# Zero fills behind weights and rows, and the routing table inside the early down product, in an FFT-convolution and mixture-of-experts kernel

## The chip, the core and the metric

One core of one Trainium2 chip runs the kernel. The metric is the device time of one execution in microseconds. The kernel before took 543.51 us, the median of three runs (543.25 to 544.37).

Engines are named TensorE (PE, with its weight loads as PEld), VectorE (DVE), ScalarE (ACT), GpSimd (POOL) and SyncE (SP, which here only issues transfers). Each works through its own instructions in order, and waits at the first one whose inputs or buffers are not ready.

## What is computed

The input is x of 8 batches x 3072 rows x 256 columns, float32. Each batch is convolved with a filter along its rows by Fourier transforms, and the result, 24576 rows, goes through a mixture of eight experts:

```python
X = np.fft.rfft(x, axis=1)
y = np.fft.irfft(X * F, n=x.shape[1], axis=1)     # attn_out
logits = rows @ w_gate                             # rows: y as (24576, 256)
expert_idx = np.argmax(logits, axis=1)             # one expert for each row
# each expert takes its first 768 rows in order; the others' output stays zero
h = np.maximum(np.einsum('ecd,edf->ecf', disp, w1), 0.0)
y = np.einsum('ecf,efd->ecd', h, w2)
out[i] = gate_w[i] * y[expert_idx[i], pos[i]]      # kept rows only
```

Eight experts take 768 rows each, so 6144 of 24576 output rows are written by an expert and all others are zero. In general the first three batches (9216 rows) fill every expert; the kernel convolves those three, and a branch on a flag convolves the others only if an expert is not yet full.

## The kernel before, in words

**Convolution of a batch.** A transform of 3072 points is done as 96 x 32. The steps `a` (input product, line 216) write ZA, `t` (transposes, line 225) write Q. Then `middle` (line 293) runs over six groups g of four frequency pairs: `b(g, h)` for the two column halves h makes a product of Q with constants on TensorE (line 242), multiplies it by the filter on VectorE (t1 and t2, line 258) and combines on GpSimd (lines 262 and 263); `catch_up` then runs `g` on the groups that are complete (line 275, with its two splits on ScalarE and VectorE, lines 278 and 279) and one step later `bi` (line 289, copied into V by ScalarE at line 291). The matmuls of line 275 in group g need the combinations of group g - 1. VectorE transposes V (`ti`, line 333), and `ai` (line 335) makes the inverse product from it in steps of three or four columns, whose results go through the tile rt (five buffers) to ybuf in memory by a store on SyncE's queue (line 350). The first of the two column halves also gives the logits L (line 349).

**Order of the work.** The instructions are written out by hand in the order in which each engine gets them. `middle` takes two lists of other work: `first`, inverse steps left over from the batch before, and `fill`, of which one entry is run between the two halves of each group from g = 1 on and one behind its `catch_up`, ten places in all. `interleave` mixes lists.

**Routing** (`route`, line 367) of a batch: counts (f0 to f5 and the matmul f6), slot numbers (`slots`), four one-hot masks (`onehot`, VectorE) and the table: 32 small matmuls (line 455) that accumulate the token of each slot, added to `tacc` (lines 460 and 461).

**Three batches.** The loop at line 700 does batch 0 and 1: four input loads for the next batch, four zero fills (`zero_out`, 2 MB each from the tile zt to the output, on SyncE), the middle, then the inverse product of this batch mixed with the input product of the next. Batch 2 follows at line 720. Its middle also carries the start of expert 0: pools for weights and rows are opened on the memory of the convolution's input (`side_ctx.close()`), w1 of expert 0 is loaded into `raw` (line 726) before the zero fills, and its splits into a high and a low part are put into fill places 0 to 3 (ScalarE and GpSimd, 512 columns each); fill place 4 holds the load of w2 of expert 0 into the same buffer (`loads[1]`, a pool of one buffer) and `early_rows`, which gathers the first 384 rows of expert 0 from batches 0 and 1 (three indirect transfers issued by GpSimd) and adds their logits; the splits of w2 (ScalarE and VectorE) follow in places 6 to 9. `early_turn` transposes the rows at the end.

**From there to the branch.** Behind batch 2's middle, up steps of expert 0 (`early`, line 754, six matmuls of line 515 each) are mixed with the inverse product (`first`, `rest`), then counts, the flag (`full_flag`: a matmul, a minimum and a cast on VectorE), slots and masks, the down product of the 384 rows (`down`, 24 matmuls of line 564 for each 128 rows, a scaled copy on ScalarE and a scatter by GpSimd), the table, and the gather of expert 0's other 384 rows (`load_rows`, line 780). All engines then load the flag into a register (line 785) and branch (line 786).

**The experts.** The loop at line 852 goes over the experts with TensorE nearly always busy: up product, down product, transposes of the next rows (`prep`), while the next expert's weights are loaded (ScalarE's queue) and split, and its rows gathered. In front of it stand `prep` of expert 0's second 384 rows and `scatter_rows`.

## Time and profile before

| | |
|---|---|
| median of three runs | 543.51 us (543.25 to 544.37) |
| the profiled execution | 547.82 us, of which 546.1 us from the first to the last instruction (the span) |
| TensorE matmuls busy | 496.4 us, 91% of the span |
| VectorE, ScalarE, GpSimd busy | 251.7, 253.0 and 238.5 us |
| mean granted TensorE clock | 0.970 of full speed |
| transfers | 81.27 MB, 149 GB/s in the mean |

Times in the profile's rows are microseconds from the span's start, and those of the prediction's steps are on the same clock. A row of a timeline gives start, duration, engine, line, operation, destination and sources, the count of merged instructions, and in brackets how long the engine had been idle and what ended that. L12 is line 12 of the kernel before. Some matmul records can be missing, and fp32 matmuls show as two records each.

### The profile page before, as it was taken

How to read it: one execution, taken by the hardware profiler on the slowest of the kernel's cores; microseconds unless marked ns; L12 is line 12 of the kernel's file. 1: busy time of each engine (PE TensorE's matmuls, PEld its weight loads, DVE VectorE, ACT ScalarE, POOL GpSimd, SP SyncE). 2: the span in 40 equal slices, each digit the busy share in tenths (PEclk: the TensorE clock that was granted, in tenths of full speed). 3: DMA queues.
4: the chain of work that ended last, by engine and by line, in shares of the span. 5: the costliest groups of instructions: out<-in, count | busy, mean ns of one | idle time of the engine just before them, and what ended most of it. 6: DMA issues, size and time to landing. Idle time of an engine off the chain costs nothing.

```text
span 546.1 us, 9913 instructions
## 1 busy us (share of the span) xinstructions
PE 496.4 (91%) x3836; PEld 489.2 (90%) x3836; DVE 251.7 (46%) x536; ACT 253.0 (46%) x599; POOL 238.5 (44%) x241
## 2 busy tenths in 40 slices
PE   7999999999997709889489999999999999999992
PEld 6889999999997709889389999999999999999992
DVE  0197743987437706757236325234242442323500
ACT  3435767356673406753154635436254362453410
POOL 2165010550106534206466946658458474582021
PEclk9999999999999958999699999999999999999997
DMA  8999662994629940161264216033170250601010
GB/s 220 306 334 406 215 184 60 314 407 134 183 59 331 401 127 1 45 180 44 71 191 151 95 50 225 30 128 118 44 231 20 80 176 32 228 24 49 0 37 22
DMA packets 52918, 81.27 MB, mean 149 GB/s; under 512 B 3968, under 2 KB 31872, under 8 KB 52736
## 3 DMA queue, kind: packets, MB, share of 16 engines
q1 hardware_dynamic: 39072, 52.90, 30.0%
q10 hardware_dynamic: 9184, 14.68, 8.3%
q0 software_dynamic: 4608, 12.98, 7.0%
q8 instruction: 32, 0.52, 0.4%
q14 instruction: 22, 0.18, 0.1%
HBM read 39.07 MB, written 41.48 MB: 148 GB/s over the span
## 4 chain that ended last, share of the span: by engine, by line
PE 37%; issue 8%; POOL 3%; DMA 2%; POOLq 0%; ACT 0%
PE ps L515 18%; PE ps L564 17%; DMA rows<-ybuf,idxg 2%; POOL y L568 2%; PE ps L486 1%; POOL rows L475 1%; POOL wbl L656 0%; POOLq L906 0%; ACT wbh L655 0%; POOL wal L656 0%; ACT h L492 0%; POOLq L568 0%; POOLq L475 0%; POOLq L785 0%; POOLq L786 0%
## 5 line engine op out<-in xcount | busy, mean ns | idle before, releaser
L564 PE MATMUL ps<-wbh,h 128*128 128x256 f32 x768 | 139.2, 281 | 0.0
L564 PEld LDWEIGHTS ps<-wbh,h 128*128 128x128 f32 x768 | 118.6, 188 | 0.0
L498 DVE SCALAR_TENSOR_TENSOR h<-ps,h 128x384 fp32r<-128x384 f32 x120 | 66.8, 558 | 91.1 <-ACT h L492 91.1
L564 PE MATMUL ps<-wbl,h 128*128 128x256 f32 x384 | 107.7, 280 | 0.0
L568 POOL DMA_INDIRECT y<-ob,idxs x48 | 49.0, 1020 | 91.2 <-ACT ob L567 89.4
L515 PE MATMUL ps<-xh,wah 128*128 128x384 f32 x256 | 86.9, 340 | 0.1
L515 PE MATMUL ps<-xl,wah 128*128 128x384 f32 x256 | 86.7, 339 | 0.0
L492 ACT ACTIVATE h<-ps 128x384 fp32r<-128x384 f32 x128 | 62.8, 493 | 51.3 <-PE ps L515 50.6
L515 PE MATMUL ps<-xh,wal 128*128 128x384 f32 x256 | 86.4, 337 | 0.0
L564 PEld LDWEIGHTS ps<-wbl,h 128*128 128x128 f32 x384 | 72.2, 188 | 0.0
L567 ACT ACTIVATE ob<-ps,gt 128x256 f32<-128x256 f32 x48 | 22.5, 473 | 82.2 <-PE ps L564 60.1
L275 PE MATMUL ps<-IG,t 128*128 128x136 f32 x288 | 40.1, 287 | 20.7 <-POOL t L263 20.7
L275 PEld LDWEIGHTS ps<-IG,t 128*128 128x128 f32 x288 | 36.6, 195 | 22.0 <-POOL t L263 21.9
L262 POOL TENSOR_TENSOR t<-t,t 128x256 f32<-128x256 f32 x33 | 24.9, 753 | 70.0 <-DVE t L258 62.0
L475 POOL DMA_INDIRECT rows<-ybuf,idxg x45 | 45.3, 1007 | 18.6 <-issue 9.5
L515 PEld LDWEIGHTS ps<-xh,wah 128*128 128x128 f32 x256 | 48.3, 189 | 0.5 <-ACT xh L492 0.5
L515 PEld LDWEIGHTS ps<-xl,wah 128*128 128x128 f32 x256 | 48.3, 189 | 0.3 <-DVE xl L500 0.3
L515 PEld LDWEIGHTS ps<-xh,wal 128*128 128x128 f32 x256 | 48.3, 189 | 0.0
L344 PE MATMUL ps<-V,AI 128*96 128x144 f32 (+1 forms) x384 | 46.6, 277 | 1.4 <-DVE V L333 1.4
L656 POOL TENSOR_TENSOR wal<-raw,wah 128x1024 fp32r<-128x1024 f32 (+1 forms) x18 | 39.0, 2182 | 19.4 <-issue 11.9
L344 PEld LDWEIGHTS ps<-V,AI 128*96 128x96 f32 x384 | 45.2, 160 | 1.9 <-ACT full L495 1.7
L500 DVE TENSOR_TENSOR xl<-ps,xh 128x384 fp32r<-128x384 f32 x32 | 16.2, 547 | 63.9 <-ACT xh L492 63.9
(118 smaller groups left out, 788.4 us busy)
## 6 DMA issues: line engine op xcount, KB each, us to landing
y<-zt SPq DMA_DIRECT2D x12, 2048.0 KB, 19.1
raw<-w ACTq DMA_DIRECT2D x14, 1024.0 KB, 7.1
xt<-x SPq DMA_DIRECT2D x20, 384.0 KB, 5.2
ybuf<-rt SPq DMA_DIRECT2D x30, 162.0 KB, 2.4
ybuf<-rt SPq DMA_DIRECT2D x24, 192.0 KB, 2.7
raw<-w SPq DMA_DIRECT2D x2, 1024.0 KB, 10.3
V<-x SPq DMA_DIRECT2D x4, 384.0 KB, 8.7
AI<-cai SPq DMA_DIRECT2D x1, 1536.0 KB, 12.5
```

The costliest lines, as they stand in the source:

```text
L262: eng.tensor_tensor(out=t1[:, :, 0, :], in0=t1[:, :, 0, :], in1=t2[:, :, 1, :], op=ALU.subtract)
L275: nc.tensor.matmul(ps[:, i * 136:(i + 1) * 136], self.ysb[(p // 4, h)][:, (p % 4) * 128:(p % 4 + 1) * 128], self.IG[:, h, :], start=True, ...
L344: nc.tensor.matmul(ps[:N1, i * w:(i + 1) * w], AI[:, n0 + i, :], V[h][:, :, n0 + i, :], start=True, stop=True)
L475: nc.gpsimd.indirect_dma_start(out=rows[:, t, :], out_offset=None, in_=yrows[:lim, :], in_offset=bass.IndirectOffsetOnAxis(ap=idx[:, j + t ...
L492: nc.scalar.activation(out=hi, in_=ps, func=f)
L498: nc.vector.scalar_tensor_tensor(out=lo, in0=ps, scalar=0.0, in1=hi.bitcast(F32), op0=ALU.max, op1=ALU.subtract)
L500: nc.vector.tensor_tensor(out=lo, in0=ps, in1=hi.bitcast(F32), op=ALU.subtract)
L515: nc.tensor.matmul(ps[:, :n * 128], w[:, kk, m * 128:(m + 1) * 128], y[:, kk, o], start=k == 0, stop=k == 5)
L564: nc.tensor.matmul(ps[:, :D], y[:, m, o], w[:, m, :], start=m == 0 and j == 0, stop=m == NF - 1 and j == 2)
L567: nc.scalar.activation(out=ob, in_=ps[:, :D], func=AF.Copy, scale=gt[:, i:i + 1])
L568: ins = nc.gpsimd.indirect_dma_start(out=out, out_offset=bass.IndirectOffsetOnAxis(ap=(idxs if ix is None else ix)[:, j:j + 1], axis=0), i ...
L656: (eng or nc.gpsimd).tensor_tensor(out=fl, in0=r, in1=fh.bitcast(F32), op=ALU.subtract)
```

## The change

Zero fills of a batch are put as single entries into places 2, 4, 6 and 8 of the middle's fill list for batches 0 and 1, and into places 4 to 7 for batch 2, behind the load of w2 and the early gather. The pools for expert 0's weights are opened, and w1 is loaded, in the loop's last pass ahead of the last six inverse steps. The index for the early scatter and the gate go into batch 2's middle. Five instead of four up steps stand before the inverse product, and five inverse steps before the slot sums; up steps 5 to 7 follow slots and masks. The down product is cut into three steps: the first stands before the table, then come the table, the flag, the gather of the next rows and a load of expert 1's w1 on SyncE, then the other two. Behind the branch the rows of expert 1 are gathered, and its w2 loaded, before expert 0's second rows are prepared. L has one buffer instead of two.

```diff
-        return p1b.tile([N1, N2, E], F32, name="L", tag="L", bufs=2)
+        return p1b.tile([N1, N2, E], F32, name="L", tag="L", bufs=1)
...
-    def down(k, fill=(), ix=None):
+    def down_steps(k, ix=None):
...
-        for i in range(n):
+        def step(i):
...
+        return [lambda i=i: step(i) for i in range(n)]
+
+    def down(k, ix=None):
+        run(down_steps(k, ix))
...
-    def load_w(e, raw, pool, parts=2, dma=None):
+    def load_w(e, raw, pool, parts=2, dma=None, boxes=()):
...
-            box = []
+            box = list(boxes[len(loads):len(loads) + 1])
 
             def load(src=src, shape=shape, box=box):
-                box.append(raw.tile(shape, F32, name="raw", tag="raw"))
-                (dma or nc.scalar).dma_start(out=box[0], in_=src)
+                if not box:
+                    box.append(raw.tile(shape, F32, name="raw", tag="raw"))
+                    (dma or nc.scalar).dma_start(out=box[0], in_=src)
...
+        def with_zeros(fill, at):
+            fill = [list(f) for f in fill] + [[] for _ in range(10 - len(fill))]
+            for i in range(nz):
+                fill[at[i % len(at)]].append(lambda: zero_out(1))
+            return fill
...
         for b in range(NB0 - 1):
             for c in range(4):
                 cv.load_x(b + 1, c)
-            zero_out(nz)
-            cv.middle(V, fill, ahead)
+            cv.middle(V, with_zeros(fill, (2, 4, 6, 8)), ahead)
...
             interleave([lambda k=k: cv.t(k) for k in range(NP // 2)], slots)
+            if b + 2 == NB0:
+                side_ctx.close()
+                w0 = ctx.enter_context(tc.tile_pool(name="w0", bufs=1, side="right"))
+                raw0 = ctx.enter_context(tc.tile_pool(name="raw0", bufs=1, side="right"))
+                ep = ctx.enter_context(tc.tile_pool(name="ep", bufs=1, side="right"))
+                loads, splits = load_w(0, raw0, w0, 4, nc.sync)
+                loads[0]()
             interleave(halves[1][:6], masks[:2])
...
         b = NB0 - 1
-        side_ctx.close()
-        w0 = ctx.enter_context(tc.tile_pool(name="w0", bufs=1, side="right"))
-        raw0 = ctx.enter_context(tc.tile_pool(name="raw0", bufs=1, side="right"))
-        ep = ctx.enter_context(tc.tile_pool(name="ep", bufs=1, side="right"))
-        loads, splits = load_w(0, raw0, w0, 4, nc.sync)
-        loads[0]()
-        zero_out(nz)
...
             gather(rows0, idx0, 0, NE, b * SEQ)
+            scatter_rows(idxs0, NE)
             nc.gpsimd.tensor_tensor(out=lg0, in0=rows0[:, :, 128:136], in1=rows0[:, :, 136:144], op=ALU.add)
 
         def early_turn():
             X[0, 0] = turn(rows0, NE, ep)
+            gate(lg0, NE, (0, 0))
...
-        cv.middle(V, fill, ahead, last=[early_turn])
+        cv.middle(V, with_zeros(fill, (4, 5, 6, 7)), ahead, last=[early_turn])
...
-        run(early[:4])
+        run(early[:5])
...
-        scatter_rows(idxs0, NE)
-        gate(lg0, NE, (0, 0))
         run(counts)
-        run(rest[:4])
+        run(rest[:5])
         sums()
-        run(rest[4:])
+        run(rest[5:])
         slots[0]()
         early_count()
-        run(early[4:6])
-        flag = full_flag()
-        run(early[6:])
         run(slots[1:])
         run(masks)
-        down((0, 0), ix=idxs0)
+        run(early[5:])
+        later = down_steps((0, 0), ix=idxs0)
+        later[0]()
         run(table)
+        flag = full_flag()
         row_of_slot(idxg, NSLOT)
         for ci in range(1, len(chunks)):
             R[0, ci] = load_rows(0, ci)
+        raw1 = raw0.tile([128, 2, FF], F32, name="raw", tag="raw")
+        nc.sync.dma_start(out=raw1, in_=w1[1].rearrange("(k p) f -> p k f", p=128))
+        run(later[1:])
...
-        for ci in range(1, NC):
-            prep((0, ci))
-        scatter_rows(idxs, NSLOT)
         for e in range(E):
...
-                loads, fill = load_w(e + 1, raw, w0 if e % 2 else w1p)
+                loads, fill = load_w(e + 1, raw, w0 if e % 2 else w1p, boxes=[raw1] if e == 0 else [])
                 for ci in range(NC):
                     R[e + 1, ci] = load_rows(e + 1, ci)
             if e == 0:
-                fill = loads + fill
+                run(loads)
+                for ci in range(1, NC):
+                    prep((0, ci))
+                scatter_rows(idxs, NSLOT)
```

## Rows read from the trace of the kernel before

**Rows 1.** Busy time by stretch: PE, PEld, DVE, ACT, POOL, PEclk, DMA share, GB/s

```profile
94.70:129.30 34.60, 34.60 (x315) 34.41 (x314) 28.32 (x52) 17.89 (x65) 16.82 (x23) 1.00 0.91 318
```

**Rows 2.** Waits of TensorE over the span: us in total, times, longest us

```profile
PE ps L275 <- POOL t L263: 20.7, 6, 15.3
```

**Rows 3.** Timeline of TensorE, second and third middle

```profile
116.24 1.55 PE L275 MATMUL ps<-IG,t 128*128 128x136 f32 x12
...
162.66 1.95 PE L242 MATMUL ps<-Bc,Q 128*128 128x128 f32 x16
...
205.04 2.64 PE L275 MATMUL ps<-IG,t 128*128 128x136 f32 x10 [15.33 <-POOL t L263]
...
221.26 0.34 PE L515 MATMUL ps<-xh,wah 128*128 128x384 f32 x1
```

**Rows 4.** Timeline of SyncE's queue around the third middle

```profile
163.90 0.45 SPq L651 DMA_DIRECT2D raw<-w  x1
164.40 15.78 SPq L129 DMA_DIRECT2D y<-zt  x4
...
187.59 2.45 SPq L651 DMA_DIRECT2D raw<-w  x1
```

**Rows 5.** Timeline of VectorE and GpSimd in the third middle

```profile
199.86 0.69 DVE L656 TENSOR_TENSOR wbl<-raw,wbh 128x512 fp32r<-128x512 f32 x1 [9.95 <-ACT wbh L655]
...
183.45 1.30 POOL L656 TENSOR_TENSOR wal<-raw,wah 128x512 fp32r<-128x512 f32 x1
...
200.14 1.29 POOL L475 DMA_INDIRECT rows<-ybuf,idx  x1 [0.30 <-issue]
203.40 0.23 POOL L734 TENSOR_TENSOR lg<-rows 128x24 f32<-128x24 f32 x1 [1.98 <-DMA rows<-ybuf,idx]
```

**Rows 6.** Timeline and line 786 around the branch

```profile
257.39 1.57 PE L455 MATMUL pr<-ohh,ol 96*128 96x96 f16 x32
260.00 1.03 POOL L475 DMA_INDIRECT rows<-ybuf,idxg  x1 [0.69 <-DVE idxg L119]
267.06 1.63 PE L486 MATMUL ps<-ident,rows 128*128 128x128 f32 x6 [8.10 <-DMA rows<-ybuf,idxg]
...
L786 PEldq COMPARE_BRANCH  x1: 3929/3929/3929, 258.6 to 258.6; - x1
```

**Rows 7.** Timeline of GpSimd, second middle, first half of the fourth group

```profile
111.35 0.74 POOL L262 TENSOR_TENSOR t<-t,t 128x256 f32<-128x256 f32 x1 [1.19 <-DVE t L258]
```

**Rows 8.** All gathers of line 475: issue to landing

```profile
DMA to landing us min/median/max: 2.8/5.3/7.0
```

**Rows 9.** Busy time by stretch, columns as in the first group

```profile
173.00:177.00 4.00, 0.93 (x8) 0.72 (x7) 3.10 (x5) 2.71 (x6) 3.45 (x4) 1.00 1.05 409
...
206.00:212.00 6.00, 6.00 (x40) 6.00 (x39) 2.53 (x5) 3.40 (x10) 1.72 (x3) 0.72 0.01 3
...
267.00:271.00 4.00, 3.87 (x13) 3.05 (x14) 1.87 (x7) 1.21 (x3) 2.00 (x2) 0.53 0.14 38
```

**Rows 10.** Timeline of VectorE and TensorE: gate, counts and flag

```profile
236.89 0.18 DVE L534 TENSOR_REDUCE gt<-lg 128x3 f32<-128x24 f32 x1 [0.29 <-ACT lg L532]
...
240.38 0.33 PE L401 MATMUL pr<-sc,tri 96*96 96x8 f32 x2 [1.62 <-DVE sc L397]
...
246.74 0.15 DVE L633 TENSOR_REDUCE cmin<-ps 1x1 f32<-1x9 f32 x1 [5.40 <-PE ps L631]
```

**Rows 11.** Chain that ended last: three down steps, sixteen up steps

```profile
282.31 8.55 PE ps L564 x72
290.86 16.77 PE ps L515 x96
```

**Rows 12.** Timeline of TensorE: preparation of expert 1's rows

```profile
281.65 0.66 PE L486 MATMUL ps<-ident,rows 128*128 128x128 f32 x4 [1.85 <-DMA rows<-ybuf,idxg]
```

**Rows 13.** Zero fills of line 129: durations, first and last start, landing

```profile
L129 SPq DMA_DIRECT2D y<-zt x12: 546/3068/12054, 26.6 to 174.9; - x12
...
DMA to landing us min/median/max: 12.2/19.1/25.3
```

More of the change, by code (lines that the diff above doesn't have):

```diff
@@ L571, in down @@
             tc.add_to_no_dep_group("scatter", ins.ins)
-            if fill:
-                fill.pop(0)()
+        return [lambda i=i: step(i) for i in range(n)]
+    def down(k, ix=None):
+        run(down_steps(k, ix))
     def scatter_rows(ix, n):
```

## The prediction

> **What bounds the kernel now.** I read the windows first. In the second batch's middle (94.70 to 129.30) TensorE is busy for all of its 34.60 us, with VectorE at 28.32 and GpSimd at 16.82 [rows 1]: there the kernel is bound by TensorE. The list of TensorE's waits then says where it is not: 20.7 us in six waits for GpSimd's line 263, one of them 15.3 [rows 2]. TensorE's timeline places it: the same middle of the third batch runs from 162.66 to 221.26, 58.6 us, with the long wait ending at 205.04 [rows 3]. SyncE's queue gives the cause: the first weights of expert 0 (raw a) go out at 163.90, then four zero fills of 2 MB, the two last stores of the batch before, and only at 187.59 the second weights (raw b) [rows 4]. VectorE gets raw b's first slice at 199.86, and GpSimd's early gather, which needs those two stores, finishes issuing at about 201.4 and has its rows at 203.40 [rows 5]. Both queues run in order, so line 262 behind the gather, and the matmuls of line 275 behind that, stand until 205.04. The second place is the branch: TensorE ends the table matmuls at 258.96, and idles 8.10 us until rows gathered from 260.00 are there [rows 6]. After the branch it is busy nearly throughout, so what moves there moves the end.
>
> **The sum's frame.** The second middle, without a wait, is the template for the third: 34.6 us, and 0.6 for six transposes of the early rows that only the third has, 35.2 in all. The third's clock is the second's plus 67.95 (162.66 less 94.71, the first product of each; the window of [rows 1] starts there). Against 58.6 that leaves 23.4 us at most.
>
> **The middle, after.** Zero fills cost SyncE only issue time, and SyncE waits for nothing in the middle, so "singly" spaces nothing: they come out back to back at the place where they stand in SyncE's queue. In the first batch this is the same place as before; in the second they merely let two stores pass. I cost both at nothing: TensorE has no wait in the second middle that could grow, and if that cover were gone, the next batch's inputs, issued behind them on the same queue, would be late by the fills' time.
>
> In the third batch raw a is issued before the last six stores and is there before its first slice, so the early wait goes. The four slices on GpSimd (line 656, 1.30 each) fit in its gaps only in part: the third and fourth come between halves of which the next, the fourth group's first half, would have started at 111.35 plus 67.95, 179.30, behind a gap of 1.19 [rows 7]. Two slices of 1.30 less that gap put it at 180.7. Raw b shares raw a's single buffer, so it can't be issued before the fourth slice ends at 180.7 either, only 7 us earlier than now; zero fills follow it. On GpSimd the half takes 2 x 0.7, then three gathers at 1.3 [rows 5], the last starting at 184.7.
>
> How long that gather lands is the largest unknown, since zero fills now run beside it and no row shows the two together. Below it is 2.8 us, above it 7.0, the ends of all gathers in this trace, many beside weight loads; I take their median, 5.3 [rows 8]. Rows at 190.0, logits 0.23, the held-back half 1.4: 191.65. The matmuls that need it stand at 116.24 in the template [rows 3], so at 184.19: a delay of **7.45 us**, with the bounds 4.95 to 9.15. Raw b, if it lands in some 9 us, blocks VectorE until about then too, but only for a half that TensorE wants 4 us later; this is hidden while raw b takes under 11. Four slices on VectorE at 0.69 [rows 5], and five small index instructions, lie mostly in that delay; I leave 0.8 for the two that fall among the last groups.
>
> Here the trace and a rule can be weighed. The row is the median of 5.3. The Trainium skill (DMA: Bandwidth & Descriptors, Queues, rings and completion order) says that each DMA engine takes its queues in turn, a packet at a time. With half of each engine, three gathers of 139 KB would be some 1 us longer than the 3.26 that the early gather needed alone, an estimate from that page's rule; the sum would be 522.2 instead of 523.2. By the same rule the rows never wait for a whole drain, as the slower rival below has it. The trace before shows no gather beside a zero fill, so it neither agrees nor differs.
>
> Clock: after 15 us of idling the granted clock was 0.72 for six microseconds, about 1.7 lost; after the 8.1 us at the branch 0.53 for four, about 1.9; around the idle 3 us in 173 to 177 it stayed at 1.00 [rows 9]. A wait of 6 to 7 us lies between: 1.0, with 0 and 2 as ends.
>
> Middle after: 35.2 + 7.45 + 0.8 + 1.0 = 44.45. **Gain 14.15.**
>
> **From the middle to the branch.** The gate of expert 0's first rows moves from 236, where it stood ahead of the routing counts, into the end of the middle. It is five VectorE instructions of 0.2 with ACT's Exp between them, which VectorE waited 0.29 for [rows 10]: 1.3. There ACT, waiting for VectorE with the Exp, holds its last copies into V, and hence the transposes and the inverse product, by that and some 0.4 of VectorE's split before it: about 1.7. One more up step covers part (sixteen take 16.77, so 1.05 [rows 11]); TensorE loses 0.7. The counts start no later than before, since the gate and four index instructions ahead of them are gone, and TensorE comes to them 1.7 later and with a fifth inverse step in front: the wait of 1.62 at 240.38 goes. The flag's matmul no longer makes VectorE wait 5.40, to 246.74 [rows 10]. Slot numbers and masks took under 10.6 us behind it (to 257.39, when TensorE began the table without a wait [rows 6]); they now start at about 241.3 and end by 251.9. TensorE reaches the table behind three inverse, three up and one down step at about 250.4, and only its last quarter needs the last mask: a wait of 0, at most 1.5. TensorE's work is unchanged in amount, so it ends at 258.0 instead of 258.96.
>
> The table now ends two down steps earlier (2.85 each, 8.55 for three [rows 11]), at about 252.2. Index 0.8 later, flag 0.35 in front of it, first gather at 253.6, rows 7.06 later as now (260.00 to 267.06): 260.6. What is late next is TensorE's branch: its compare-and-branch stood for 3929 ns, hidden now by the rows [rows 6]. From 258.0, TensorE resumes at 261.9 instead of 267.06: **gain 5.15**. Below 3.9 the rows bound it at 260.6 (1.3 more gain); if code comes slower, say 2 us, so much less. Its idling falls from 8.1 to 3.9, so I take 1.0 of the 1.9 of clock back: **gain 1.0**, bounds 0 and 1.9.
>
> **Behind the branch.** The 1 MB of expert 1's first weights is issued on SyncE behind the last store and lands beside down steps; it delays nothing, and ACT issues one load fewer, but that one ahead of its first split (0.4, inside the idle time). Gathers for expert 1 stand ahead of the first preparation. They started 1.4 us after TensorE's restart; GpSimd must now issue two scatters first and let them land, so they start 1.6 to 1.8 after. The wait of 1.85 at 281.65 [rows 12] therefore stays; bounds: all of it gained, or 0.5 lost.
>
> **Sum.** 14.15 + 5.15 + 1.0 = 20.3. The profiled execution has a span of 546.1 and a time of 547.82; its span would be 525.8. Measured runs have a median of 543.51, 4.3 below the profiled time; the waits are the same in both, so 543.5 less 20.3 is **523.2 us**.
>
> **Rivals.** *Rows late by part of the drain.* If rows or raw b take what raw b took before, 187.59 to 199.86, 12.3 us [rows 4, 5], the delay is 14.45 and the clock costs 2: middle gain 6.15, total 12.3, 531.2. For it: they share the DMA engines with 8 MB. Against: the zero fills start after them. Chance 0.15.
>
> *Nothing collides.* Rows in 3.3, no clock loss at either wait, no wait at 281.65: 17.15 + 5.15 + 1.9 + 1.85 = 26.1, 517.4. For it: neither wait would be over 5 us; against: GpSimd's order alone holds TensorE 5 us. Chance 0.13.
>
> *Slower: the gather waits for the whole drain.* Place: GpSimd's queue in the third middle. Zero fills start at 181.7; first to last took 10.5 (164.4 to 174.9), and one lands 19.1 (median) to 25.3 us after issue [rows 13]: 211 to 217, 26 to 32 after the last gather's start. The delay is then 28.3 to 34.5, the middle 66 to 72 instead of 58.6, and with 6.15 gained later the kernel is 1.5 to 7.7 slower, about 548. It decides from a landing of 24.7 us on. For it: nothing but the fills' own times; against: gathers beside weight loads never took over 7.0 [rows 8]. Chance 0.04.
>
> *It doesn't do what it says:* raw b can't go before the fourth slice, and if that came much later than 180.7, or raw a waited for the memory it takes over, the long wait would stay whole and the branch would be all: 537 at best, and with a slower fetch or clock next to no change. Chance 0.02.
>
> **How the numbers follow.** Forecast 0.66. The range, 516 to 531.5, reaches from the second rival to the first with the bounds of the landing, the clock and the branch; beyond it are the two last rivals and some of the first. About 0.2% (1 us) is what a measurement here can tell: faster 0.94, within it 0.02, slower 0.04.
>
> **What would show it.** Right: the third middle some 44 us, one wait of 5 to 8 us on line 263 in it, no wait of ACT for raw a, the gather's rows within 7 us; no wait at the inverse product's counts; TensorE's restart after the branch bound by its own branch, near 4 us. Wrong: rows or raw b landing after 10 us, a wait of TensorE on VectorE's masks before the table, TensorE held after the branch by rows, or a new wait of the last batch's stores behind the fills.

## The result, and the profile after

The kernel after the change takes **530.2 us** (median of 4 runs, 528.1 to 531.49) against 543.43 for the kernel before, measured beside it: ratio 0.9749, interval 0.9713 to 0.9786. That is 13.2 us less. The forecast was 523.2 us, a gain of 20.3: the sign held, the range (to 531.5) held by 1.3 us, and the size was half as large again as measured. The profiled execution is the fastest of the four, 528.1 us with a span of 526.4.

The stages are cut at four events, read from TensorE's timelines: the third middle's first product of line 242, the first up product behind it (line 515), the first transposes of the next rows behind the branch, and the end of the transposes ahead of the expert loop's first down product.

```
execution        to middle  middle  to restart  to loop   loop    span
before, 1st        162.66    58.60     45.80     15.25   263.79   546.1
before, again      161.78    55.51     45.56     14.94   263.31   541.1
after, 1st         161.43    47.08     42.48     13.13   262.28   526.4
after, again       160.94    46.95     41.73     13.28   262.30   525.2
```

In the second execution of each (runs b_again and a_again below) the spans differ by 15.9: 8.56 in the middle, 3.83 up to the restart, 1.66 from there to the loop, 1.0 in the loop and 0.84 ahead of the middle. The first profiles of each differ by 19.7, near the forecast, but this agreement misleads: the first profile of before (547.82 us) was 4.3 above its median, and that of after 2.1 below its own. The middle of before's first profile was 3.1 longer than in its second.

The middle, in the list of TensorE's waits (columns as in [rows 2]) and its timeline:

```profile
PE ps L275 <- POOL t L263: 7.2, 4, 5.3
PE ps L486 <- DMA rows<-ybuf,idxg: 5.4, 1, 5.4
```

```profile
175.14 2.02 PE L242 MATMUL ps<-Bc,Q 128*128 128x128 f32 x16 [0.78 <-DVE t L258]
...
179.12 0.50 PE L275 MATMUL ps<-IG,t 128*128 128x136 f32 x2 [0.80 <-POOL t L263]
...
182.95 0.39 PE L289 MATMUL ps<-yh,BIh 128*128 128x272 f32 x1 [0.81 <-DVE t L258]
...
192.17 2.63 PE L275 MATMUL ps<-IG,t 128*128 128x136 f32 x10 [5.33 <-POOL t L263]
```

The 20.7 us of waits for line 263 [rows 2] are 7.2 now, and the 15.33 that ended at 205.04 [rows 3] is 5.33 and ends at 192.17. SyncE's queue shows why: the first weights now go out ahead of the last stores of the batch before, and the second ahead of the fills, at 156.39 and 180.34 in place of 163.90 and 187.59 [rows 4].

```profile
156.39 0.41 SPq L655 DMA_DIRECT2D raw<-w  x1
158.00 9.02 SPq L350 DMA_DIRECT2D ybuf<-rt  x8
180.34 0.40 SPq L655 DMA_DIRECT2D raw<-w  x1
180.78 14.41 SPq L129 DMA_DIRECT2D y<-zt  x4
```

Behind raw b the four fills go out back to back, as the forecast said. Beside them GpSimd gathers the early rows (its timeline, to be read against [rows 5]):

```profile
181.86 1.18 POOL L475 DMA_INDIRECT rows<-ybuf,idx  x1 [0.17 <-DVE idxs L585]
183.34 1.01 POOL L475 DMA_INDIRECT rows<-ybuf,idx  x1 [0.31 <-issue]
184.65 1.00 POOL L475 DMA_INDIRECT rows<-ybuf,idx  x1 [0.30 <-issue]
190.53 0.23 POOL L744 TENSOR_TENSOR lg<-rows 128x24 f32<-128x24 f32 x1 [4.89 <-DMA rows<-ybuf,idx]
190.72 0.71 POOL L262 TENSOR_TENSOR t<-t,t 128x256 f32<-128x256 f32 x1
191.40 0.71 POOL L263 TENSOR_TENSOR t<-t,t 128x256 f32<-128x256 f32 x1
```

GpSimd stands 4.89 us at the small add of the logits (line 744), with lines 262 and 263 queued behind it and TensorE behind those. The rows are there 5.88 us after the last gather's start.

The second place is the branch (TensorE's and GpSimd's timelines, then instructions of line 798: duration in ns min/median/max, first and last start):

```profile
238.97 0.51 PE L455 MATMUL pr<-ohh,ol 96*128 96x96 f16 x8 [0.66 <-DVE ohh L447]
...
250.99 1.66 PE L486 MATMUL ps<-ident,rows 128*128 128x128 f32 x6 [5.44 <-DMA rows<-ybuf,idxg]
...
243.26 1.00 POOL L475 DMA_INDIRECT rows<-ybuf,idxg  x1 [0.31 <-issue]
244.57 1.03 POOL L569 DMA_INDIRECT y<-ob,idxs  x1 [0.30 <-issue]
247.10 1.01 POOL L569 DMA_INDIRECT y<-ob,idxs  x1 [1.51 <-ACT ob L568]
```

```profile
L798 PEldq COMPARE_BRANCH  x1: 3372/3372/3372, 243.8 to 243.8; - x1
...
L798 PEldq EVENT_SEMAPHORE  x1: 51/51/51, 247.3 to 247.3; - x1
L798 POOLq COMPARE_BRANCH  x1: 53/53/53, 247.4 to 247.4; - x1
...
L798 POOLq INC_SWDGE_SEM  x1: 368/368/368, 250.6 to 250.6; - x1
```

TensorE idles 5.44 where it idled 8.10 [rows 6]. Its own branch was over at 247.3, though, and the next rows had been asked for by 244.3. What ends just ahead of the restart is GpSimd's last record at the branch, a semaphore record of 0.37 from 250.6 (a semaphore is a counter by which an engine or a transfer tells the others that it is done). GpSimd issues the last scatter at 247.10 and branches at 247.4; its first record behind the branch comes at 250.1, and this one at 250.6. In the trace's semaphore updates, the counter on which TensorE's first transposes wait, that of the first gather of the next rows, rises for the last time before the restart at 250.85, inside this record, although the last of these gathers had landed at 247.1. That is why the list of waits names the rows' transfer. In the ten traces that have all scatters of the early rows ahead of the branch, those of before too, the restart follows this record's end within 0.2 us. In before it stands just ahead of the restart at 267.06 (instructions of line 786):

```profile
L786 POOLq INC_SWDGE_SEM  x1: 368/368/368, 266.5 to 266.5; - x1
```

### The profile page after: what moved, and what is told of

Read it like the earlier page. It is cut to its first block, busy times and chain, and to the rows that moved or that the text cites. A ratio compares the mean times of both kernels' runs of the same rounds, so it can differ in the third digit from the quotient of the medians.

```text
span 526.4 us, 9909 instructions
## 1 busy us (share of the span) xinstructions
PE 496.0 (94%) x3836; PEld 490.4 (93%) x3836; DVE 252.7 (48%) x536; ACT 250.6 (48%) x599; POOL 237.0 (45%) x241
## 4 chain that ended last, share of the span: by engine, by line
PE 73%; issue 9%; DVE 5%; POOL 5%; DMA 4%; ACT 2%; POOLq 0%; ACTq 0%; SPq 0%; DVEq 0%
PE ps L515 20%; PE ps L565 18%; PE ps L222 9%; PE ps L344 8%; PE ps L275 5%; PE ps L242 4%; PE ps L289 4%; PE ps L231 3%; DMA y<-ob,idxs 2%; POOL y L569 2%; PE ps L486 1%; DVE t L258 1%; DMA rows<-ybuf,idx 1%; DVE V L333 1%; DMA xt<-x 1%
## 5 line engine op out<-in xcount | busy, mean ns | idle before, releaser
L498 DVE SCALAR_TENSOR_TENSOR h<-ps,h 128x384 fp32r<-128x384 f32 x120 | 65.2, 556 | 92.9 <-ACT h L492 85.5
L492 ACT ACTIVATE h<-ps 128x384 fp32r<-128x384 f32 x128 | 61.3, 496 | 53.1 <-PE ps L515 43.1
L569 POOL DMA_INDIRECT y<-ob,idxs x48 | 47.7, 994 | 84.1 <-ACT ob L568 80.4
L475 POOL DMA_INDIRECT rows<-ybuf,idxg x45 | 45.3, 1007 | 19.2 <-issue 12.5
L278 ACT CAST yh<-ps 128x408 fp32r<-128x408 f32 x48 | 24.0, 499 | 45.3 <-PE ps L275 45.3
## 6 DMA issues: line engine op xcount, KB each, us to landing
y<-zt SPq DMA_DIRECT2D x12, 2048.0 KB, 19.7
```

The lines of the kernel that those rows point to most:

```text
L278: nc.scalar.copy(fh[:, o], ps[:, :408])
L475: nc.gpsimd.indirect_dma_start(out=rows[:, t, :], out_offset=None, in_=yrows[:lim, :], in_offset=bass.IndirectOffsetOnAxis(ap=idx[:, j + t ...
L492: nc.scalar.activation(out=hi, in_=ps, func=f)
L498: nc.vector.scalar_tensor_tensor(out=lo, in0=ps, scalar=0.0, in1=hi.bitcast(F32), op0=ALU.max, op1=ALU.subtract)
L569: ins = nc.gpsimd.indirect_dma_start(out=out, out_offset=bass.IndirectOffsetOnAxis(ap=(idxs if ix is None else ix)[:, j:j + 1], axis=0), i ...
```

## Experiments

Times are medians. Each group of runs was measured beside the kernel before, and ratios are to that; "base" is the kernel after the change unless another is named.

**a_again, lg_late, no_fills, down2.** The base once more, and three edits of it:

> The changed kernel once more, to see where runs that lie between 528 and 531.5 us differ, and what in the first profile of the kernel before was peculiar to that execution. If the waits differ (third middle, branch), the middle and the stretch to the branch move by 1 to 3 us against 47.1 and 42.5 us, and the expert loop does not. If TensorE's pace differs, the loop's period for an expert (34.97 us in the first profile) moves by 0.1 to 0.3 us and the waits stay.

529.0 us (526.9 to 530.1), ratio 0.9722 (0.9687 to 0.9757), 15.8 below the 544.81 of before beside it. The waits are those of the first profile, 5.18 in the middle and 4.68 at the branch (5.33 and 5.44 there).

lg_late, the add of the logits from GpSimd to VectorE:

```diff
         scatter_rows(idxs0, NE)
-        nc.gpsimd.tensor_tensor(out=lg0, in0=rows0[:, :, 128:136], in1=rows0[:, :, 136:144], op=ALU.add)
...
         X[0, 0] = turn(rows0, NE, ep)
+        nc.vector.tensor_tensor(out=lg0, in0=rows0[:, :, 128:136], in1=rows0[:, :, 136:144], op=ALU.add)
         gate(lg0, NE, (0, 0))
```

> The add of the early logits goes from GpSimd, behind the gather, to VectorE, behind the early transposes; GpSimd no longer stands for the rows. If the held-back half on GpSimd is what TensorE waits for (my theory), GpSimd is free 4.9 us earlier, the wait of 5.3 us on line 263 falls to under 1.5 and the time falls by 4 to 6 us, with the clock's part. If raw b on VectorE sets it (rival), the wait falls by at most 1.5 us, for VectorE has that slice at 187.8 already.

**523.6 us**, ratio 0.9609 (0.9576 to 0.9642), 5.4 below a_again. GpSimd goes on with line 262 as soon as its gathers are issued, and TensorE's long wait is gone (both timelines):

```profile
185.34 1.00 POOL L475 DMA_INDIRECT rows<-ybuf,idx  x1 [0.30 <-issue]
186.36 0.74 POOL L262 TENSOR_TENSOR t<-t,t 128x256 f32<-128x256 f32 x1
...
187.82 1.43 PE L275 MATMUL ps<-IG,t 128*128 128x136 f32 x10 [0.29 <-POOL t L263]
```

The middle is 40.28 us, 6.67 less than in a_again, and the granted clock over it 1.00 instead of 0.93 (windows by stage, columns as in [rows 1]):

```profile
162.13:202.41 40.28, 36.98 (x320) 35.46 (x319) 35.26 (x63) 22.42 (x71) 25.96 (x30) 1.00 0.64 222
```

So the rest of the middle's wait is the order on GpSimd's queue; no transfer had to become faster for it to go. The rival, the second weights on VectorE, allowed 1.5 us at most.

no_fills leaves out the four zero fills of the third middle, so a third of the output's zeros is not written:

```diff
-        cv.middle(V, with_zeros(fill, (4, 5, 6, 7)), ahead, last=[early_turn])
+        cv.middle(V, fill, ahead, last=[early_turn])
...
-        zero_out(len(zfill))
```

> The four zero fills of the third middle are left out (a third of the output is not zeroed). If the fills lengthen the gather's landing (5.9 us from the last issue, against 3.3 before), it falls to about 3.5, the wait of 5.3 to about 3, and the time by 2 to 3 us. If the landing is the gather's own, time and wait stay within 1 us.

525.3 us, ratio 0.964 (0.9599 to 0.968), 3.7 below a_again. The rows land 3.15 us after the last gather's start instead of 5.88, and TensorE's wait falls from 5.33 to 2.57 (GpSimd's and TensorE's timelines):

```profile
184.42 1.00 POOL L475 DMA_INDIRECT rows<-ybuf,idx  x1 [0.30 <-issue]
187.57 0.23 POOL L744 TENSOR_TENSOR lg<-rows 128x24 f32<-128x24 f32 x1 [2.14 <-DVE wbl L660]
...
189.20 1.62 PE L275 MATMUL ps<-IG,t 128*128 128x136 f32 x10 [2.57 <-POOL t L263]
```

The fills beside the gather cost 2.7 us of its landing, not a whole drain (one fill lands 19.1 us after its issue in the median [rows 13]). The Trainium skill (DMA: Bandwidth & Descriptors, Queues, rings and completion order) lets each DMA engine take its queues in turn, which the forecast had turned into an estimate of about 1 us: the direction agrees, the measured 2.7 is more than twice that.

down2 puts two of the three down steps ahead of the table, so that the next rows are asked for 2 us later against the rest:

```diff
-        later[0]()
+        run(later[:2])
...
-        run(later[1:])
+        run(later[2:])
```

> Two instead of one of the three down steps stand ahead of the table, so the rows behind the branch are gathered 2.8 us later, while the last scatter and the branch keep their places. If GpSimd's own way through the branch (last scatter, code for the branch's target, its semaphore count) sets TensorE's restart (my theory), the gap of 5.4 us stays within 0.5 us and so does the time. If the rows' landing sets it (as the list of waits says), the gap grows to about 8 us and the time by 2 to 3 us.

528.4 us, ratio 0.9706 (0.9665 to 0.9748): not to be told from a_again. With later gathers the restart stayed where it was, 41.96 us behind the end of the middle (42.48 and 41.73 in the two profiles of after). The last of these rows lands at 249.0, 2.3 us before the restart at 251.31, so in this kernel their landing does not set it.

**b_again, mid_only, end_only, no_branch.**

> The kernel before, profiled once more. Its first profile (547.82 us) lies above the median of its runs. If that execution was merely slow in TensorE's pace (my theory), the expert loop's period is now nearer the 34.97 us of the kernel after than the 35.16 of the first profile, and the third middle (58.6 us) and the stretch from it to the first preparation (45.8 us) stay within 1 us. If the slower pace belongs to the kernel before, the period is 35.1 to 35.2 again and part of the change's gain lies in the expert loop.

544.3 us, ratio 1.0006 (0.998 to 1.0032). The expectation failed: the middle did not stay within 1 us, it is 55.51 and not 58.60, while the loop's period for an expert, 35.1, is nearer to the 35.2 of the first profile than to the 35.0 of after (TensorE's timeline, the middle's one wait above 1 us and the early one):

```profile
172.95 0.96 PE L275 MATMUL ps<-IG,t 128*128 128x136 f32 x6 [0.56 <-POOL t L263]
...
200.96 2.63 PE L275 MATMUL ps<-IG,t 128*128 128x136 f32 x10 [14.63 <-POOL t L263]
```

In the first profile the early wait, for raw a, was 3.08. It varies from execution to execution: raw a, with the fills behind it on the same queue, landed 8.9 us after its issue in the first profile and 6.4 here. Of the 15.33 the wait here still has 14.63.

mid_only takes the first half of the change (fills, pools and early weight, index for the early scatter stays late), end_only the second (everything from the gate's move on but the middle's order):

```diff
 mid_only, against after
-            gate(lg0, NE, (0, 0))
...
-        run(early[:5])
+        run(early[:4])
...
-        later[0]()
+        down((0, 0), ix=idxs0)
...
 end_only, against after
-            cv.middle(V, with_zeros(fill, (2, 4, 6, 8)), ahead)
+            zero_out(nz)
+            cv.middle(V, fill, ahead)
...
+        loads[0]()
+        zero_out(nz)
```

> Only the first half of the change: fills behind weights and rows, early pools and first weights; gate, up steps, flag, table, down steps and what stands behind the branch as before. By the two traces the middle is worth 11.5 us and nothing of the rest remains: about 11 to 12.5 us below the kernel before. If the halves depend on each other (rival: the later part gains only because the middle ends earlier), the gain is over 14 or under 9.

535.5 us, ratio 0.9861 (0.982 to 0.9903).

> Only the second half: gate, up steps, table inside the down product, rows gathered first, expert 1's weights early; the third middle's fills and loads as before. By the two traces it is worth 3.4 us to the branch and 2.5 us at the preparation of expert 1's rows, less 0.4 of clock: 4.5 to 6 us below the kernel before. If the halves depend on each other, under 3 or over 8.

539.7 us, ratio 0.9918 (0.9891 to 0.9944).

The halves give 8.6 and 4.4 below the 544.05 of before beside them, 13.0 in all. Both miss what was expected, 11 to 12.5 and 4.5 to 6, and the first is even below the 9 that was to be a sign that the halves depend on each other. The traces speak against that: the middle is 47.30 us in mid_only, as with both halves (47.08 and 46.95), and what was too large is the 11.5 expected of it, which had been taken from the long first profile of before. The middle's half keeps the old waits at the counts (1.62) and at the branch (7.8), the end's half keeps the long wait in the middle (14.46). So the two places look separate; their 13.0 is close to the 13.2 of the whole change, and below the 15.8 of a_again, which were not measured side by side with them.

no_branch leaves out the reading of the flag, the branch and the work that it guards:

```diff
-        least = nc.values_load(flag[0:1, 0:1], min_val=0, max_val=NTOK)
-        with tc.If(least < cap):
...
```

> The flag is computed, but the branch and the work it guards are left out (never needed for this input). If GpSimd's way through the branch is what TensorE waits for behind the down steps, the gap of 5.4 us falls to what the rows' landing alone needs, under 3 us, and the time by 2.5 to 5 us with the clock. If the rows' landing sets the gap, it stays at 5 us or more and the time within 1 us.

534.7 us, ratio 0.9831 (0.9794 to 0.9869): *slower* than with the branch, where 2.5 to 5 us less or no change had been expected. TensorE's transposes came at 246.55 after a wait of 0.38, so the rows had landed; then it stood 11.04 for ScalarE's copies (timelines of TensorE, ScalarE and GpSimd):

```profile
246.55 0.66 PE L486 MATMUL ps<-ident,rows 128*128 128x128 f32 x4 [0.38 <-DMA rows<-ybuf,idxg]
258.25 0.69 PE L515 MATMUL ps<-xh,wah 128*128 128x384 f32 x1 [11.04 <-ACT xh L492]
...
256.72 0.42 ACTq L655 DMA_DIRECT2D raw<-w  x1
257.71 0.87 ACT L492 ACTIVATE xh<-ps 128x384 fp32r<-128x384 f32 x2 [10.43 <-issue]
...
254.15 1.03 POOL L569 DMA_INDIRECT y<-ob,idxs  x1 [0.30 <-issue]
```

The load of expert 1's second weight stands ahead of these copies on ScalarE's queue and is issued only 2.6 us after the last scatter, which without the branch is queued behind six gathers on GpSimd. In the trace the load waits for that scatter's landing, at 256.5. In the kernel after, the last scatter stands ahead of these gathers and has landed (250.3) before the load goes out at 251.37, so this wait doesn't show. The run was meant to price the branch and didn't; it does show that the next rows were there by 246.55.

**lg_late_2, late_down, late_both.** With lg_late as the base: late_down moves the second and third down steps behind the branch, late_both also puts the load of expert 1's second weight behind the turn of the next rows.

```diff
 late_down
-        run(later[1:])
         top_ctx.close()
...
             if e == 0:
+                run(later[1:])
                 run(loads)
...
 late_both
                 run(later[1:])
-                run(loads)
                 for ci in range(1, NC):
                     prep((0, ci))
+                run(loads)
```

> The kernel with the logits' add on VectorE once more, as the base of the two runs beside it: 521 to 525 us, and the restart behind the branch again within 0.2 us of the end of GpSimd's semaphore record there, some 5 us after TensorE's last down product.

524.35 us, ratio 0.9605 (0.956 to 0.9651): as lg_late was.

> The base with the second and third down steps (products, scaling and scatter) moved behind the branch, ahead of the turn of the next rows. Theory: GpSimd's way through the branch, behind the last two scatters, sets the restart; without them GpSimd enters the branch some 2 to 3 us earlier against TensorE's last product before it, so TensorE stands 3.4 to 4 us (its own branch) in place of 5.3, and the 5.7 us of down products lie over what the next rows still lack. Then 1.5 to 3.5 us below the base, about 521. Rival: the landing of the next rows or the branch itself sets it, and the down steps only change their place: within 0.7 us of the base. Third: the two scatters now fall on GpSimd's and the queue's time at the first up steps and the weight that shares the wait comes later: 1 to 2 us given back at expert 1.

523.6 us, ratio 0.9606 (0.9572 to 0.9639), so not to be told from its base. TensorE still stands 5.05, but for another reason: its own branch now waits for the flag, which TensorE reads at 234.6 together with SyncE, ScalarE and VectorE, and then takes 3.37, to 238.6; ScalarE is through at 238.8, and the list names it (instructions of line 798, TensorE's timeline):

```profile
L798 PEldq COMPARE_BRANCH  x1: 3372/3372/3372, 235.2 to 235.2; - x1
...
L798 POOLq INC_SWDGE_SEM  x1: 328/328/328, 242.2 to 242.2; - x1
```

```profile
238.91 0.58 PE L565 MATMUL ps<-wbh,h 128*128 128x256 f32 x1 [5.05 <-ACTq L798]
```

GpSimd's record is 3.1 us earlier than in lg_late_2 (242.2 against 245.3) and hidden behind the down products, as the theory had it. What it gives is used up: the branch no longer runs beside down products, and these now run at a clock of 0.50 after the idle time (239 to 243; 1.00 from 244 on). Counted from the middle's start, the expert loop's first down product begins 96.2 us later here, 96.1 and 97.3 in the two runs of the base: between nothing and 1.1 gained, less than the theory's lower end of 1.5.

> As the run before, and the load of expert 1's second weight on ScalarE's queue put behind the turn of the next rows in place of ahead of it. If that load's wait for the scatter holds up ScalarE's copies of the turned rows (as in the run without the branch, where it stood 11.0 us), the stretch from the first transposes behind the branch to the first up product shortens by up to 3 us; if nothing waits there, the time is that of the run before within 0.5 us.

523.2 us, ratio 0.9606 (0.9561 to 0.9651): within 0.5 of the run before. The load held nothing up there.

**scat_late.** lg_late with products and scaling where they were, and the two scatters held until behind the branch (the results wait in a dead buffer). The load of expert 1's second weight follows behind them; in lg_late it goes out at 245.35, after the restart at 244.97, so its move cannot explain a shorter wait there.

```diff
-            ob = sm["p"].tile([128, D], F32, name="ob", tag="ob", bufs=4)
+            if hold is not None and i:
+                ob = rows0[:, i, :D]
+            else:
+                ob = sm["p"].tile([128, D], F32, name="ob", tag="ob", bufs=4)
...
+            if hold is not None and i:
+                hold.append(scatter)
+            else:
+                scatter()
...
-                run(loads)
                 for ci in range(1, NC):
                     prep((0, ci))
+                run(held)
+                run(loads)
```

> The kernel with the logits' add on VectorE, its second and third down products and their scaling ahead of the branch as before, but the two scatters of their results held until the next rows are turned behind the branch (the results wait in a dead part of the early rows' buffer), and the load of expert 1's second weight behind them. Theory: GpSimd's way through the branch, late because it dispatches these two scatters first, holds TensorE's restart; TensorE's own branch ended 1.8 us after its last product there (242.0 against 240.27) and GpSimd's record only at 245.7. So TensorE's wait of 5.5 us falls to 2 to 3 us, the first up product behind the branch comes 2.5 to 3.5 us earlier, and the time is 2 to 3.5 us below that kernel's 523.6 to 524.4. Rival: the landing of the next rows sets it: the wait stays over 4.5 us and the time within 0.7 us.

**521.8 us** (520.3 to 524.3), ratio 0.9573 (0.9546 to 0.96). GpSimd branches at 236.3 in place of 241.4, its record ends at 242.1, and TensorE restarts after 3.08 instead of 5.49 (instructions of line 808, the branch's line in this kernel; TensorE's timeline):

```profile
L808 POOLq EVENT_SEMAPHORE  x5: 17/43/43, 238.9 to 241.7; - x5
...
L808 POOLq COMPARE_BRANCH  x1: 53/53/53, 236.3 to 236.3; - x1
...
L808 ACTq COMPARE_BRANCH  x1: 45/45/45, 240.4 to 240.4; - x1
...
L808 POOLq INC_SWDGE_SEM  x1: 328/328/328, 241.8 to 241.8; - x1
L808 ACTq EVENT_SEMAPHORE  x1: 17/17/17, 242.8 to 242.8; - x1
```

```profile
242.87 0.33 PE L486 MATMUL ps<-ident,rows 128*128 128x128 f32 x1 [3.08 <-ACTq L808]
244.62 1.33 PE L486 MATMUL ps<-ident,rows 128*128 128x128 f32 x5 [1.42 <-issue]
```

The wait of 3.08 is just above the 2 to 3 us that was expected. It is ScalarE that comes last now: it scales the last down product, branches at 240.4 and is through at 242.8. The rows as cause of the longer wait are ruled out: they are gathered at the same place as in lg_late_2, where the last of them landed at 241.8 (237.99 plus 3.8), 4 us before the restart. Of the 2.4 us, 1.42 come back as a stand behind the first transposes that the trace puts down to nothing ("issue"); the first up product is about 1 us earlier, counted from the end of the last product ahead of the branch (6.2 us against 7.2 and 7.3), less than the 2.5 to 3.5 expected. The time is 1.8 and 2.5 below the two runs of lg_late. Since these were not measured side by side and the intervals of the ratios overlap (0.9546 to 0.96 and 0.9576 to 0.9642), this gain is likely, not settled. It is the fastest of all the kernels here, some 23 us below before.

What GpSimd's record waits for is not the branch alone. In lg_late GpSimd branches at 240.8 and has its first records behind the branch from 243.4 on, but the record ahead of the restart starts only at 244.5 (instructions of line 798):

```profile
L798 POOLq EVENT_SEMAPHORE  x5: 17/43/43, 243.4 to 243.8; - x5
...
L798 POOLq INC_SWDGE_SEM  x1: 368/368/368, 244.5 to 244.5; - x1
```

The last scatter, started at 240.45, lands 4.1 us later, at 244.5. Seven of the ten traces are like this: the record starts within 0.1 us of the landing of the last transfer that GpSimd issued ahead of the branch. That is a scatter in lg_late, lg_late_2, down2 and end_only, and the last gather of the next rows in before, b_again and mid_only (262.66 plus 3.8, 266.5, in before). In after, a_again and no_fills the transfer had landed 0.3 to 0.9 us earlier, and the record follows 0.4 us behind the first one behind the branch. In scat_late GpSimd is past its branch at 238.9, and its records stop until 241.6, when the last gather has landed. So when GpSimd is through depends on its branch (2.6 to 3.3 us to the first record behind it) and on the landing of what it issued last. Holding the scatters back brings both forward, and no run separates them.

## Why the prediction was right in sign and too large

**The frame.** "The waits are the same in both" failed: they are not the same in the profiled execution and in the median run. The profiled execution was 4.3 above the median, and in another execution of before the middle was 3.1 shorter, 2.5 of it in the early wait for raw a (3.08 and 0.56). The forecast subtracted the whole of this longer execution's waits from the median. Against the second execution that is 3.1 of the 20.3; since that one (542.81) was itself 1.5 below the median of its runs, the median run may lie between the two.

**The middle.** The mechanism held: raw a ahead of the stores, no wait for it; raw b 18.9 us into the middle (forecast 18.0, 180.7 less 162.66); fills that space nothing out; one long wait on line 263, and line 262 behind the gather as its cause, which lg_late showed. Sizes were off by 2.5 in all, 47.0 for 44.45. The delay of the held-back half was 9.21 (192.17 less 161.43, less the template's 21.53) for 7.45: landing 5.88 for 5.3, and the last gather 23.2 us into the middle where 22.0 was forecast. Most of the latter is the fourth slice on GpSimd, which ended 18.9 us into the middle and not 18.0. The index instructions ahead of the gathers, which the forecast costed as small, take up to 1.25 us on VectorE, but hold the first gather by only 0.17. They also bring TensorE the wait of 0.81 at 182.95, which mid_only, without them at this place, does not have; it falls ahead of the long wait, which is 7.08 in mid_only, and seems to cost nothing here, since the middle of mid_only is no shorter.

```profile
179.08 1.25 DVE L583 TENSOR_SCALAR te<-tacc 128x3 f32<-128x3 f32 x1
180.37 0.65 DVE L584 TENSOR_TENSOR te<-te,tf 128x3 f32<-128x3 f32 x1
181.06 0.66 DVE L585 CAST idxs<-te 128x3 int32<-128x3 f32 x1
```

The rest, 0.8, fits the clock, which was 0.55 in the mean (1.00 is 2.4 GHz, 0.50 is 1.2) for the six microseconds behind the wait. For it 1.0 us was set aside; in lg_late, where the clock stays at 1.00, the middle is 6.67 shorter than in a_again, 1.8 more than the long wait lost (5.18 less 0.29):

```profile
192.00:198.00 6.00, 5.83 (x28) 5.84 (x29) 1.99 (x4) 3.03 (x10) 2.85 (x5) 0.55 1.05 409
```

**To the restart.** The waits ahead of the branch came as forecast: none at the counts, 0.66 at the masks (0 to 1.5 expected). The step that failed is "what is late next is TensorE's branch". That branch, 3372 ns, was over at 247.3, since it runs ahead while the last down products are still being worked off. Late next was GpSimd, which branches behind the last scatter, and whose record behind the branch also waits for that scatter's landing (250.3 in after, 0.3 before the record). The forecast had moved two scatters to that place and counted them only behind the branch. The trace of before could have told: the same record stood just ahead of its restart, there behind the landing of the next rows. The forecast gain of 5.15 and 1.0 of clock became 3.8 (3.3 in the first pair). No clock came back: the window behind the restart is at 0.50, as it was at 0.53 [rows 9].

```profile
251.00:255.00 4.00, 3.81 (x12) 2.93 (x13) 1.79 (x7) 1.11 (x3) 2.04 (x2) 0.50 0.55 174
```

The Trainium skill (Runtime: NRT & Kernel Launch, Instruction fetch mechanics) has a taken branch fetch its target before execution goes on, when the target is not in the window already fetched. That fits the 2.4 to 4.0 us that TensorE, ScalarE and GpSimd each need from their branch to their next record in these traces; VectorE needs 0.6, and no run separates the fetch from the rest. In scat_late the last engine to branch, ScalarE at 240.4, is also the last to be through, at 242.8.

**Behind the branch.** That the wait of 1.85 stays failed as a step, in the kernel's favour: the gathers for expert 1 land in time, and twelve transposes run without a wait. They start 1.5 us after the restart, as forecast, but the last lands 2.8 us after its issue (259.10) where it took 6.6 in before (issued at 275.00): there expert 1's two weight loads went out among these gathers, and now both are out before them. No run tests this by itself.

```profile
262.65 1.47 PE L486 MATMUL ps<-ident,rows 128*128 128x128 f32 x12
```

This is most of the 1.7 to 2.1 gained from the restart to the loop. The loop itself gave 1.0 to 1.5 and the stages ahead of the middle 0.8 to 1.2. For neither had the forecast a term, and no run here isolates a cause. Part of the loop's share varies with the execution: its period for an expert is 35.2 and 35.1 in the two of before and 35.0 in both of after, but also 34.96 in lg_late and 35.07 in lg_late_2, the same kernel. The terms close: 20.3 less 3.1 (frame), 2.5 (middle) and 2.3 (branch), plus 1.7, 1.0 and 0.8, is 15.9, the difference of the second pair of profiles. The 13.2 between the medians first measured is 2.7 less, and 15.8 was measured with a_again; nothing here explains that scatter.

**The rivals.** Slower was ruled out: the rows landed in 5.88 us and not in 26 to 32, and by no_fills the fills are 2.7 of that. "Nothing collides" was wrong for the middle and right for the wait of 1.85. "Rows late by part of the drain" gave 531.2, close to the measured 530.2, but not by its mechanism: the rows took 5.88, not 12.3, and raw b 6.8. "It doesn't do what it says" came true in nothing: raw b went out 0.9 later than forecast, and the long wait shrank. What stays open is why the runs of one kernel scatter by 3 to 6 us, what the stand of 1.42 in scat_late is, and how much of GpSimd's way through the branch is the branch and how much the landing.

## What to carry to other kernels

Look at what is queued behind a waiting instruction before looking at the transfer it waits for: one small add on GpSimd, moved to another queue, was worth 5.4 us, more than taking the zero fills away. At a branch, find for each engine when it gets there and when it is through, and what it issued last ahead of it: here TensorE went on only when GpSimd was through, with its last transfer landed, while the list of waits named rows that had landed almost 4 us before. Before a profiled execution's waits are subtracted from a median, ask which of them vary from execution to execution.

## What was not expected of the hardware

TensorE's branch, 3.4 to 4.0 us long in all traces that have it, starts 1.7 us before the last product ahead of it ends (243.8 and 245.5 in the kernel after), so part of it is hidden behind products that are queued already; with the flag late (late_down) it isn't. GpSimd's last record at the branch starts in no trace before GpSimd's last transfer ahead of it has landed, a scatter too, whose result TensorE does not read (lg_late, both at 244.5). Leaving the branch out made the kernel 5.7 us slower than a_again (not measured side by side); the trace puts it down to an order of two queues that does no harm with the branch. Small index instructions of 3 elements per partition took 0.65 to 1.25 us on VectorE beside GpSimd's work, and 0.15 just before; the same ones took 0.16 to 0.17 in before. Each of the three ends within 0.1 us of the end of the GpSimd instruction beside it (180.31, 181.00 and 181.68). No edit tests this.
